# Token lists of the last two batches, and the pace at which w_out is converted in the last layers

## The chip, the cores and the metric

One core of a Trainium2 chip runs the whole program. Its engines are TensorE (PE, matrix products), VectorE (DVE), ScalarE (ACT), GpSimd (POOL), and SyncE (SP), which here only issues DMA. Each engine executes its instructions in the order in which they stand in its own list, and engines wait for each other by semaphores. The metric is the device time of one execution in microseconds (us). TensorE runs at a clock that the chip grants; in the profile "PEclk" 1.00 stands for 2.4 GHz and 0.50 for 1.2 GHz.

## What is computed

Three stages follow each other: attention with pooled keys, a mixture of experts in which every token goes to one expert of limited capacity, and a two-layer network with a squared relu.

```python
# q, k, v: (B=4, H=8, S=576, D=64); keys and values averaged over 8 positions
attn = softmax(q @ k_pooled.T / 8) @ v_pooled
x = attn.transpose(0, 2, 1, 3).reshape(2304, 512)
# moe: E=8 experts, cap=576 tokens each, 512 -> 1024 -> 512
logits = x @ w_gate
expert_idx = argmax(logits, axis=1)          # first come, first served up to cap
h = np.maximum(np.einsum('ecd,edf->ecf', disp, w1), 0.0)
y = np.einsum('ecf,efd->ecd', h, w2)
out[i] = gate_w[i] * y[expert_idx[i], pos[i]]   # tokens that were kept, else 0
# moe2: w_in 512 x 2048 and w_out 2048 x 512 arrive as 64-bit floats
r = np.maximum(x @ w_in, 0.0)
g = s * (r * r) + b
return (g @ w_out).astype(np.float32)
```

## The kernel before, in words

**Order.** The program is scheduled by hand: the order in which the Python code emits instructions is the order of each engine's list. Where several strands of work are woven together, generators are advanced by step tables; no scheduler moves anything afterwards. Every float32 product is made as three matmuls of high and low parts ("h" and "l" tiles): the high part is a cast, the low part a subtraction.

**Attention and routing.** A batch's 576 tokens are five tiles of 128 (the last is half full), in all N = 20 tiles. For a group of tiles `route` (L329) finds each token's expert as a one-hot tile `roh` (L352), and PE then counts the tokens of each expert with matmuls of `roh` and a triangular matrix (L368 to L376, the "ranks"). The rank of a token in its expert is `rr` (L384). `tail` (L397) turns ranks into list positions: `rslot` (L402), `rkey` (L404), the token numbers `tok` (an iota on POOL, L401, masked on DVE, L405), and the one-hot tiles `ohq` (L408, L412) and `ohp` (L414). `add_lists` (L429) multiplies `ohp` and `ohq` on PE (L434) and adds the result to the lists of tokens per expert, `u_lists` (L437). The last batch is routed in two groups: its first three tiles, then its last two. A pick (L689 on PE, L690 and L691 on DVE) reads the list of the next unit of expert work, and POOL gathers that unit's tokens with indirect DMA (`xg`, L938). Expert units of 288 tokens begin while attention still runs: `beside` (L974) lays their layer 1 (L961) and layer 2 (L1108) between the last attention tiles. `w1l` (L930) is the low part of an expert's weights, made on POOL and DVE.

**Conversion of 64-bit weights.** `Weights64` (L850) turns a piece of 128 rows and 512 columns of 64-bit floats into float32 in four steps, each with one DVE instruction: a shift (L868, a tensor_scalar), then three scalar_tensor_tensor instructions (L871, L873, L877). The absolute value `c_u` that the fourth needs is made on ACT (L870) in the second step. The second step of the next piece also finishes the piece before: ACT casts the high part (L1386) and DVE subtracts (L1387); the third step adds the piece into a running sum of all pieces, `raw[3]` (L1392). `w_in` is converted this way earlier, with raw pieces in three tiles `c_raw`; `w_out` has 16 pieces, `wo0` to `wo15`: 14 in a first series of 59 steps, then two in a series of 11.

**Last layers** (`last_layers`, L1362). Units of CU = 256 tokens go through layer 1 (16 column groups f, 12 matmuls of 256 columns each, L1034) and layer 2 (L1432, per f six matmuls of 512 columns). After layer 1 of an f, `square` (L1411 relu on ACT, L1412 on DVE) frees the PSUM bank, and `parts` makes `gh` on ACT (L1426) and `gl` on POOL, or on DVE for every third f (L1427). There are eight banks for unit 0 and four for unit 1. Units 0 and 1 run as a pair (`pair`, L1460) in this order:

- `first(0, 0, 16)`: layer 1 of unit 0, one conversion step per f; in the middle the input of unit 1 is split (`y1l`, L1027);
- `first(1, 0, 7)`: layer 1 of unit 1 up to f = 6 (HEAD = 7), one step per f;
- `second(0, 0, 7)` and `second(1, 0, 7)`: layer 2 of both for f = 0 to 6, two steps per f;
- the rest of `first(1, ...)`, the steps that the first series still has, then the rest of `second` for both with two steps per f.

Then units 2 and on follow one after the other. The first four f of unit 0 (EARLY = 4) are put before the pair, behind the last small expert.

**The hand-over.** The last small expert ends in `last` (L1297): its output `yo` goes from ACT to DRAM by a DMA that SP issues (L1113), and SP then issues the loads of `wo` (L1458). The `wo` tiles lie in pools that are only free once the expert stage has ended.

## Time and profile before

| | |
|---|---|
| three runs | 657.16, 660.01, 661.97 us (median 660.01) |
| the profiled execution | 664.05 us, of which the span of instructions is 662.3 us |
| PE busy | 592.1 us (89%) |
| DVE, ACT, POOL busy | 365.5 us (55%), 253.6 us (38%), 265.8 us (40%) |
| clock granted to PE, mean over the span | 0.952 |
| stages by the trace | attention to about 150 us, experts to about 335 us, last layers from there |

PE is busy nearly all the time, so the time is made of PE's work, of the places where PE waits, and of the stretches in which PE works at half its clock. A row of a timeline gives the start, the busy time, the engine, the line, the operation with its tiles, and in square brackets how long the engine sat idle before and what ended that.

### The profile page before, as it was taken

What the parts mean: (1) busy time and instruction counts of PE and PEld (TensorE: products, weight loads), DVE (VectorE), ACT (ScalarE), POOL (GpSimd) and SP (SyncE); (2) the same over time, 40 slices, a digit from 0 to 9 for tenths busy, and PEclk for the clock granted to TensorE, in tenths of its full rate; (3) what the DMA queues carried; (4) which work ended last, traced back from release to release, by engine and by line L of the source; (5) the groups of instructions that cost most, each with busy time, mean ns of one, the idle gap of its engine ahead of it and who ended that gap; (6) DMA issues with size and microseconds to landing.
All of it is one profiled execution on the core that took longest, in us unless ns stands there. A gap on an engine that the chain in (4) does not pass through costs nothing. (4 is left out here: it accounts for less than half of the span.)

```text
span 662.3 us, 11174 instructions
## 1 busy us (share of the span) xinstructions
PE 592.1 (89%) x4005; PEld 549.5 (83%) x4005; DVE 365.5 (55%) x889; ACT 253.6 (38%) x620; POOL 265.8 (40%) x384
## 2 busy tenths in 40 slices
PE   5787888769899979997897996999999999999884
PEld 5787777669899979996897976889899899898784
DVE  4688798867968956661639999603312021131140
ACT  1354555436456645442336524304125033042130
POOL 5658434715154716012214301305725145144281
PEclk8799899879999989996999898999999999999998
DMA  8989665645649894844548111017300101000000
GB/s 165 199 183 190 163 195 171 215 126 197 232 155 295 282 309 148 282 135 156 169 142 350 38 33 32 1 33 286 111 17 1 49 17 29 29 9 2 35 2 20
DMA packets 67951, 86.12 MB, mean 130 GB/s; under 512 B 24713, under 2 KB 40073, under 8 KB 67856
## 3 DMA queue, kind: packets, MB, share of 16 engines
q1 hardware_dynamic: 57696, 71.34, 35.9%
q10 hardware_dynamic: 7712, 6.84, 3.4%
q0 software_dynamic: 2448, 6.82, 3.1%
q8 instruction: 42, 0.69, 0.5%
q14 instruction: 53, 0.43, 0.2%
HBM read 68.09 MB, written 17.58 MB: 129 GB/s over the span
## 5 line engine op out<-in xcount | busy, mean ns | idle before, releaser
L1432 PE MATMUL bank<-wo,gh 128*128 128x512 f32 (+1 forms) x412 | 119.3, 374 | 1.2 <-ACT wo L1386 1.0
L1427 POOL TENSOR_TENSOR gl<-rt,gh 128x256 fp32r<-128x256 f32 (+1 forms) x96 | 72.6, 761 | 110.8 <-ACT gh L1426 64.7
L1432 PEld LDWEIGHTS bank<-wo,gh 128*128 128x128 f32 x412 | 74.9, 188 | 15.1 <-ACT wo L1386 1.4
L1432 PE MATMUL bank<-wo,gl 128*128 128x512 f32 (+1 forms) x206 | 76.8, 373 | 0.0
L930 POOL TENSOR_TENSOR w1l<-kraw,w1h 128x128 fp32r<-128x128 f32 x96 | 52.6, 582 | 50.7 <-ACT w1h L923 50.6
L1108 PE MATMUL bank<-hs,w2h 128*128 128x288 f32 (+1 forms) x308 | 68.5, 311 | 4.7 <-issue 4.3
L1439 DVE SCALAR_TENSOR_TENSOR raw<-bank,sb,c_u 128x512 f32<-128x512 f32 (+1 forms) x14 | 9.9, 710 | 85.5 <-PE bank L1432 85.5
L1108 PEld LDWEIGHTS bank<-hs,w2h 128*128 128x128 f32 x308 | 50.7, 192 | 5.6 <-issue 5.1
L1411 ACT ACTIVATE rt<-tq 128x256 f32<-128x256 f32 (+1 forms) x26 | 9.5, 367 | 113.5 <-PE tq L1034 91.3
L1108 PE MATMUL bank<-hs,w2l 128*128 128x288 f32 (+1 forms) x148 | 44.7, 302 | 0.0
L1432 PEld LDWEIGHTS bank<-wo,gl 128*128 128x128 f32 x206 | 38.8, 188 | 6.8
L1412 DVE SCALAR_TENSOR_TENSOR rt<-bank,rt 128x256 f32<-128x256 f32 (+1 forms) x53 | 21.2, 401 | 38.3 <-ACT rt L1411 37.9
L1426 ACT CAST gh<-rt 128x256 fp32r<-128x256 f32 (+1 forms) x96 | 36.6, 381 | 6.5 <-DVE rt L1412 6.5
L938 POOL DMA_INDIRECT xg<-xd,u_idx x23 | 25.4, 1104 | 30.0 <-DVE r L288 16.7
L1440 POOL DMA_INDIRECT out_dram<-raw,it x12 | 12.0, 1001 | 62.6 <-DVE raw L1439 62.1
L1411 ACT ACTIVATE rt<-bank 128x256 f32<-128x256 f32 (+1 forms) x60 | 22.3, 371 | 35.4 <-PE bank L1034 27.0
L228 PE MATMUL sc<-kbd,qT 128*128 128x144 f32 (+1 forms) x152 | 25.4, 316 | 5.6 <-DVE r L286 3.6
L1412 DVE SCALAR_TENSOR_TENSOR rt<-tq,rt 128x256 f32<-128x256 f32 (+1 forms) x24 | 9.6, 400 | 36.3 <-ACT rt L1411 36.3
L1108 PEld LDWEIGHTS bank<-hs,w2l 128*128 128x128 f32 x148 | 28.4, 192 | 0.0
L228 PEld LDWEIGHTS sc<-kbd,qT 128*128 128x128 f32 (+1 forms) x152 | 21.9, 201 | 7.7 <-issue 5.1
L934 DVE TENSOR_TENSOR w2l<-vraw,w2h 128x512 fp32r<-128x512 f32 x39 | 27.4, 702 | 1.2 <-ACT w2h L933 0.5
L961 PE MATMUL bank<-xs,w1h 128*128 128x288 f32 (+1 forms) x120 | 26.1, 303 | 2.1 <-DVE hs L964 2.1
(485 smaller groups left out, 1705.0 us busy)
## 6 DMA issues: line engine op xcount, KB each, us to landing
kraw<-in_moe_w_dram SPq DMA_DIRECT2D x14, 1024.0 KB
vraw<-in_moe_w_dram SPq DMA_DIRECT2D x14, 1024.0 KB
wo<-in_moe_w_out_dram SPq DMA_DIRECT2D x16, 512.0 KB
c_raw<-in_moe_w_in_dram ACTq DMA_DIRECT2D x13, 512.0 KB
kraw<-in_k_dram SPq DMA_DIRECT2D x8, 576.0 KB
out_dram<-c_u SPq DMA_DIRECT2D x1, 4608.0 KB
q<-in_q_dram SPq DMA_DIRECT2D x16, 256.0 KB
xd<-xr SPq DMA_DIRECT2D x16, 256.0 KB
```

The costliest lines, as they stand in the source:

```text
L228: nc.tensor.matmul(sc[:n, p // 2, p % 2 * 144:p % 2 * 144 + 144], lhsT=q[:, p, :n], rhs=kbd[b % 2][:, p], start=True, stop=True)
L930: eng.tensor_sub(self.w1l[:, i, z], self.w1(i)[:, z], self.w1h[:, i, z])
L934: eng.tensor_sub(self.w2l[i], self.w2r[:, i], self.w2h[i])
L938: self.nc.gpsimd.indirect_dma_start(out=dst, out_offset=None, in_=self.xd[:have], in_offset=bass.IndirectOffsetOnAxis(ap=idx[:n], axis=0), ...
L961: self.nc.tensor.matmul(p, lhsT=l[:, f, k], rhs=r[k], start=n == 0, stop=n == 3 * KD - 1)
L1108: nc.tensor.matmul(py[d][:, :v.n], lhsT=l[f][:, d * P:d * P + P], rhs=r[f], start=f == 0 and i == 0, stop=f == KF - 1 and i == 2)
L1411: nc.scalar.activation(r, p, AF.Relu)
L1412: nc.vector.scalar_tensor_tensor(out=p if inside else r, in0=p, scalar=0.0, in1=r, op0=ALU.max, op1=ALU.mult)
L1426: nc.scalar.copy(h[:, :n], r)
L1427: (nc.gpsimd if p is None else nc.vector).tensor_sub(l[:, :n], r, h[:, :n])
L1432: nc.tensor.matmul(p[:, c], lhsT=g[:, j * P:j * P + P], rhs=wo[f][:, z, c], start=f == 0 and i == 0, stop=f == KF2 - 1 and i == 2)
L1440: i = nc.gpsimd.indirect_dma_start(out=dst, out_offset=bass.IndirectOffsetOnAxis(ap=ids, axis=0), in_=o[:, c], in_offset=None, bounds_chec ...
```

## The change

**Routing.** The token numbers of all tiles are made once at the start (`toks`), so the iota in `tail` goes. The tail of batch 2 no longer hands its lists over at the first opportunity but waits until tile N - 1; its `add_lists` takes the place of the pick for unit 1, and that pick and its gather move one place on, behind the ranks of the last two tiles. The ending loop gives the second share of side work to the first of the last ranks, not to the second.

**w_in and w_out.** The raw tiles of `w_in` and the first three `wo` pieces share three tiles of a new pool `keep`, so these pieces can be loaded before the expert stage has ended. The last raw piece of `w_in` is loaded at step 51, not 54. In `last`, ACT takes over SP's part in storing the last small expert's output (it loads the address into a register of its own and issues the DMA), and the split of unit 0's input comes two f later.

**Last layers.** For pieces 0 to 2 the absolute value is made on DVE and the high part (and the start of the running sum) on POOL, so that ACT has no part in them. The first 12 steps stand ahead of unit 0's layer 1. Beside it a step is made every second f; in the first half of layer 2 one step per f, where there were two. The steps made by the last square of unit 1 are then 12 + 8 + 7 + 14 + 9 = 50 of 70 (before: 16 + 7 + 28 + 8 = 59); 20 stand behind it (before: 11).

```diff
@@ constants
+        toks = one.tile([P, B, NB], F32, name="toks")
+        nc.gpsimd.iota(toks, pattern=[[S, B], [P, NB]], base=0, channel_multiplier=1, allow_small_or_imprecise_dtypes=True)
@@ tail
-            nc.gpsimd.iota(tok, pattern=[[P, w]], base=b * S + t0 * P, channel_multiplier=1, allow_small_or_imprecise_dtypes=True)
...
-            v.scalar_tensor_tensor(out=tok, in0=r, scalar=float(cap), in1=tok, op0=ALU.is_lt, op1=ALU.mult)
+            v.scalar_tensor_tensor(out=tok, in0=r, scalar=float(cap), in1=toks[:, b, t0:t1], op0=ALU.is_lt, op1=ALU.mult)
...
+            while b == B - 2 and now[0] < N - 1:
+                yield True
             yield from window()
             add_lists(b, at_pe[0])
@@ ending loop
-                    for _ in range(2 if ranks == 1 else 1):
+                    for _ in range(2 if ranks == 0 else 1):
@@ Weights64.step
-                self.nc.scalar.activation(u, t.bitcast(F32)[:, :, 1], AF.Abs)
+                if i < self.alone:
+                    v.tensor_scalar(out=u.bitcast(I32), in0=hi, scalar1=0x7FFFFFFF, scalar2=None, op0=ALU.bitwise_and)
+                else:
+                    self.nc.scalar.activation(u, t.bitcast(F32)[:, :, 1], AF.Abs)
@@ Experts
-            self.c_raw.append(self.m.tile([P, DM, 2], I32, name=f"c_raw{i - 9}"))
+            self.c_raw.append(self.keep.tile([P, DM, 2], I32, name=f"c_raw{i - 9}"))
@@ conv (w_in)
-                    if pos[0] == 3 or pos[0] % 4 == 2 and pos[0] > 6:
-                        self.load_raw(max(3, pos[0] // 4 + 2), queue)
+                    if pos[0] in (3, MARK - 1) or pos[0] % 4 == 2 and 6 < pos[0] < MARK:
+                        self.load_raw(KF2 - 1 if pos[0] == MARK - 1 else max(3, pos[0] // 4 + 2), queue)
@@ last
+            nc.vector.memset(self.ids_half[:, 0:1], 0)
+            nc.scalar.copy(self.ids_half[:, 1:2], self.ids_half[:, 0:1])
+            col = nc.values_load(ti[0:1, 2, self.t.NV + s:self.t.NV + s + 1], engines=[ET.Activation], min_val=0, max_val=T)
...
-                if early and f in (4, 5):
+                if early and f in (6, 7):
...
-            store_small(s)
+            store_y(sid(s), yo(s % 2, SM), SM, nc.scalar, col)
@@ last_layers
-    gl = pool.tile([P, KF2, CU], F32R, name="gl")
-    wo = [pool.tile([P, DM, 2], I32, name=f"wo{i}") for i in reversed(range(KF2))][::-1]
+    gl = side.tile([P, KF2, CU], F32R, name="gl")
+    FIRST = len(x.c_raw)
+    place_out = lambda i, shape, dt: x.keep.tile(shape, dt, name=f"c_raw{i}") if i < FIRST else side.tile(shape, dt, name=f"wo{i}")
+    wo = [place_out(i, [P, DM, 2], I32) for i in reversed(range(KF2))][::-1]
...
-        nc.scalar.copy(w[:, 0], f)
+        if i < FIRST:
+            nc.gpsimd.tensor_copy(w[:, 0], f)
+        else:
+            nc.scalar.copy(w[:, 0], f)
...
-            nc.scalar.copy(raw[3], f)
+            nc.gpsimd.tensor_copy(raw[3], f)
@@ pair
-                conv(1, steps_of_first)
+                conv(u or f % 2, steps_of_first)
...
-                conv(2, end)
+                conv(1 if f < HEAD else 2, end)
...
+        conv(4 * FIRST)
+        nc.gpsimd.memset(onesf, 1.0)
         first(0, 0, KF2, ps)
```

The order in three places, all on DVE. The first is the routing of the last batch: from the list position of its first three tiles to the one-hot tile `roh` of its last two (`xr`, `r`, `lt`, `lg` belong to the attention of the last tile). Before:

```order
L404 TENSOR_SCALAR rkey_1698<-rslot_1696 128x3
L405 SCALAR_TENSOR_TENSOR tok_1699<-rr_1691,tok_1699 128x3
L294 TENSOR_REDUCE lg_174<-lt 64x8
L408 TENSOR_TENSOR ohq<-rkey_1698,q_179 128x144
L409 TENSOR_SCALAR rlo_1697<-rkey_1698 128x3
L411 TENSOR_TENSOR rlo_1697<-rlo_1697,rslot_1696 128x3
L412 TENSOR_TENSOR ohq<-ohq,tok_1699 128x144
L414 TENSOR_TENSOR ohp<-rlo_1697,p_180 128x288
L324 TENSOR_SCALAR xr_176<-xr_176,rgs_1659 128x512
L338 TENSOR_REDUCE rmx_1718<-lg_174 128x2
```

The same place of the change, with the rows that lead to `roh`:

```order
L290 RECIPROCAL r<-r 64x8
L292 TENSOR_TENSOR xr_179<-sc,r 64x512
L294 TENSOR_TENSOR lt<-sc,r 64x64
L296 TENSOR_REDUCE lg_177<-lt 64x8
L326 TENSOR_SCALAR xr_179<-xr_179,rgs_1632 128x512
L340 TENSOR_REDUCE rmx_1695<-lg_177 128x2
L343 TENSOR_TENSOR rd_1697<-lg_177,rmx_1695 128x16
L348 SCALAR_TENSOR_TENSOR rval_191<-rd_1697,rev 128x2x8
L351 TENSOR_REDUCE rvm_1701<-rval_191 128x2
L354 TENSOR_TENSOR roh_1703<-rval_191,rvm_1701 128x16
```

The tail's instructions no longer stand among them: they come some 20 rows further on, behind `roh` and behind the ranks.

The second place is the start of unit 0's squares on DVE, behind the last rows of the expert stage. Before, conversion and squares alternate from the first square on (`rt`, `bank`, `tq` and `misc` are the squares' tiles):

```order
L1412 SCALAR_TENSOR_TENSOR rt_1968<-tq,rt_1968 128x256
L868 TENSOR_SCALAR c_f_16943<-wo_16963 128x512
L1412 SCALAR_TENSOR_TENSOR rt_1969<-misc,rt_1969 128x256
L871 SCALAR_TENSOR_TENSOR c_f_16943<-wo_16963,c_f_16943 128x512
L1412 SCALAR_TENSOR_TENSOR bank_1942<-bank_1942,rt_1970 128x256
L873 SCALAR_TENSOR_TENSOR c_f_16943<-wo_16963,c_f_16943 128x512
```

In the change 18 conversion rows stand ahead of the first square; the last six of them and the first three squares:

```order
L871 TENSOR_SCALAR c_f_17063<-c_raw_17081 128x512
L874 TENSOR_SCALAR c_u_17065<-c_raw_17081 128x512
L877 SCALAR_TENSOR_TENSOR c_f_17063<-c_raw_17081,c_f_17063 128x512
L1400 TENSOR_TENSOR c_raw_17124<-c_f_17064,c_raw_17124 128x512
L879 SCALAR_TENSOR_TENSOR c_f_17063<-c_raw_17081,c_f_17063 128x512
L1405 TENSOR_TENSOR raw_1963<-raw_1963,c_f_17064 128x512
L883 SCALAR_TENSOR_TENSOR c_f_17063<-c_u_17065,c_f_17063 128x512
L1425 SCALAR_TENSOR_TENSOR rt_1968<-tq,rt_1968 128x256
L1425 SCALAR_TENSOR_TENSOR rt_1969<-misc,rt_1969 128x256
L871 TENSOR_SCALAR c_f_17064<-wo_17080 128x512
L1425 SCALAR_TENSOR_TENSOR bank_1942<-bank_1942,rt_1970 128x256
```

So the first square now waits for the conversion of three pieces, and fewer conversion rows lie between the squares that follow.

The third place is DVE behind the last square of unit 1 (its last `gl` is the row with `raw<-bank,raw`), while PE does the second half of layer 2. Before, 12 rows finish the last two pieces:

```order
L1427 TENSOR_TENSOR raw_16984<-bank_1942,raw_16984 128x256
L868 TENSOR_SCALAR c_f_16943<-wo_17514 128x512
L871 SCALAR_TENSOR_TENSOR c_f_16943<-wo_17514,c_f_16943 128x512
L873 SCALAR_TENSOR_TENSOR c_f_16943<-wo_17514,c_f_16943 128x512
L877 SCALAR_TENSOR_TENSOR c_f_16943<-c_u_16945,c_f_16943 128x512
L868 TENSOR_SCALAR c_f_16944<-wo_17516 128x512
L871 SCALAR_TENSOR_TENSOR c_f_16944<-wo_17516,c_f_16944 128x512
L1387 TENSOR_TENSOR wo_17702<-c_f_16943,wo_17702 128x512
```

In the change 11 rows stand between that `gl` and the last two pieces:

```order
L1440 TENSOR_TENSOR raw_17104<-bank_1942,raw_17104 128x256
L879 SCALAR_TENSOR_TENSOR c_f_17063<-wo_17071,c_f_17063 128x512
L1405 TENSOR_TENSOR raw_1963<-raw_1963,c_f_17064 128x512
L883 SCALAR_TENSOR_TENSOR c_f_17063<-c_u_17065,c_f_17063 128x512
L871 TENSOR_SCALAR c_f_17064<-wo_17070 128x512
L877 SCALAR_TENSOR_TENSOR c_f_17064<-wo_17070,c_f_17064 128x512
L1400 TENSOR_TENSOR wo_17786<-c_f_17063,wo_17786 128x512
L879 SCALAR_TENSOR_TENSOR c_f_17064<-wo_17070,c_f_17064 128x512
L1405 TENSOR_TENSOR raw_1963<-raw_1963,c_f_17063 128x512
L883 SCALAR_TENSOR_TENSOR c_f_17064<-c_u_17065,c_f_17064 128x512
L1400 TENSOR_TENSOR wo_17792<-c_f_17064,wo_17792 128x512
L1405 TENSOR_TENSOR raw_1963<-raw_1963,c_f_17064 128x512
```

The pieces `wo12` and `wo13` are thus finished here too, ahead of `wo14` and `wo15`.

## Rows read from the trace of the kernel before

**Rows 1.** The page: busy time of each engine (share of the span), instructions

```profile
PE 592.1 (89%) x4005; PEld 549.5 (83%) x4005; DVE 365.5 (55%) x889; ACT 253.6 (38%) x620; POOL 265.8 (40%) x384
```

**Rows 2.** Timeline of DVE in the routing: start, busy, instruction, idle before

```profile
130.49 0.15 DVE L404 TENSOR_SCALAR rkey<-rslot 128x3 f32<-128x3 f32 x1
134.75 0.16 DVE L405 SCALAR_TENSOR_TENSOR tok<-rr,tok 128x3 f32<-128x3 f32 x1 [4.11 <-POOL tok L401]
...
136.08 0.48 DVE L324 TENSOR_SCALAR xr<-xr,rgs 128x512 f32<-128x512 f32 x1
...
137.29 0.17 DVE L352 TENSOR_TENSOR roh<-rval,rvm 128x16 bf16<-128x16 f32 x1
```

**Rows 3.** Timeline of PE in the routing

```profile
119.33 1.15 PE L434 MATMUL o<-ohp,ohq 128*48 128x96 f32 x10 [1.00 <-DVE ohp L414]
...
131.86 0.29 PE L961 MATMUL misc<-xs,w1l 128*128 128x288 f32 x1
137.52 0.20 PE L368 MATMUL o<-roh,tri 128*128 128x16 bf16 x1 [5.37 <-DVE roh L352]
...
152.29 0.41 PE L952 MATMUL tq<-ident,xg 96*128 96x96 f32 x3
```

**Rows 4.** Tile xg: gathers (ns min/median/max, first and last start), and issue to landing

```profile
L938 POOL DMA_INDIRECT xg<-xd,u_idx x23: 923/985/2147, 105.0 to 302.8; - x23
...
DMA to landing us min/median/max: 3.1/5.0/7.1
```

**Rows 5.** Windows of 2 us: busy of PE, PEld, DVE, ACT, POOL; PEclk; DMA

```profile
366.00:368.00 2.00, 2.00 (x11) 2.00 (x11) 1.54 (x5) 1.08 (x4) 0.74 (x1) 0.50 0.64 194
```

**Rows 6.** Timeline of SP at the hand-over to the last layers

```profile
328.09 1.04 SPq L1022 DMA_DIRECT2D it<-idc  x1
...
339.62 3.93 SPq L1458 DMA_DIRECT2D wo<-in_moe_w_out_dram  x6
```

**Rows 7.** Timeline of DVE at the hand-over, and beside POOL's gl

```profile
332.60 1.43 DVE L1027 TENSOR_TENSOR yhl<-yr,yhl 128x256 fp32r<-128x256 f32 x4 [7.66 <-ACT yhl L1026]
...
344.11 0.43 DVE L868 TENSOR_SCALAR c_f<-wo 128x512 int32<-128x512 int32 x1 [6.63 <-DMA wo<-in_moe_w_out_dram]
...
349.62 1.23 DVE L1387 TENSOR_TENSOR wo<-c_f,wo 128x512 fp32r<-128x512 f32 x1
```

**Rows 8.** Timeline of DVE: conversion alone, and behind the last square

```profile
400.03 0.69 DVE L1387 TENSOR_TENSOR wo<-c_f,wo 128x512 fp32r<-128x512 f32 x1 [0.24 <-ACT wo L1386]
400.63 0.68 DVE L873 SCALAR_TENSOR_TENSOR c_f<-wo,c_f 128x512 int32<-128x512 int32 x1
...
418.10 0.42 DVE L1412 SCALAR_TENSOR_TENSOR rt<-bank,rt 128x256 f32<-128x256 f32 x1 [0.33 <-ACT rt L1411]
418.44 0.41 DVE L1427 TENSOR_TENSOR raw<-bank,raw 128x256 fp32r<-128x256 f32 x1
...
426.53 0.69 DVE L1387 TENSOR_TENSOR wo<-c_f,wo 128x512 fp32r<-128x512 f32 x1 [0.80 <-issue]
```

**Rows 9.** Timeline of PE in the last layers

```profile
346.27 0.40 PE L1034 MATMUL tq<-yhl,w2h 128*128 128x256 f32 x2
...
363.85 0.58 PE L1034 MATMUL tq<-y1l,w1h 128*128 128x256 f32 x1 [2.63 <-DVE y1l L1027]
...
406.10 0.39 PE L1034 MATMUL bank<-y1h,w2h 128*128 128x256 f32 x1 [3.79 <-DVE rt L1412]
...
409.56 0.58 PE L1034 MATMUL tq<-y1h,w2h 128*128 128x256 f32 x1 [1.77 <-DVE gl L1427]
```

**Rows 10.** The chain that ended last: start, length, engine, tile, line

```profile
417.64 24.59 PE bank L1432 x108
442.24 1.42 PE tq L1034 x12
```

**Rows 11.** Timeline of POOL: a gl beside DVE, a 512-column op on POOL

```profile
295.42 1.27 POOL L1046 TENSOR_TENSOR w2l<-raw,w2h 128x512 fp32r<-128x512 f32 x1 [5.65 <-ACT w2h L1045]
...
349.37 0.92 POOL L1427 TENSOR_TENSOR gl<-rt,gh 128x256 fp32r<-128x256 f32 x1 [1.01 <-ACT gh L1426]
```

More of the change, by code (lines that the diff above doesn't have):

```diff
@@ L852, with __init__ @@
 class Weights64:
-    def __init__(self, nc, pieces, raw, out, f, u, late=None):
-        self.nc, self.raw, self.out, self.f, self.u, self.late = nc, raw, out, f, u, late
+    def __init__(self, nc, pieces, raw, out, f, u, late=None, alone=0):
+        self.nc, self.raw, self.out, self.f, self.u, self.late, self.alone = nc, raw, out, f, u, late, alone
         self.pieces, self.total = pieces, 4 * pieces + (3 if late else 2)
@@ L887, in __init__ @@
             self.n, self.xh, self.xl, self.hh, self.hl = n, x[:KD], x[KD:2 * KD], h[:KF], h[KF:2 * KF]
-    def __init__(self, nc, tc, c, a, left, m, xd, idc, yt, hist, cap, capp):
+    def __init__(self, nc, tc, c, a, left, keep, m, xd, idc, yt, hist, cap, capp):
         self.__dict__.update({k: v for k, v in locals().items() if k != "self"})
@@ L1076, in main @@
         queue = nc.scalar
-        c_f = [one.tile([P, DM], I32, name=f"c_f{i}") for i in range(2)]
+        c_f = [left.tile([P, DM], I32, name=f"c_f{i}") for i in range(2)]
         def out(i, f):
@@ L1086, in main @@
         cv = Weights64(nc, KF2, lambda i: self.c_raw[i % 3], out, lambda i: self.raw[i].bitcast(I32) if i < KF else c_f[i % 2],
-                       [one.tile([P, DM], F32, name=f"c_u{i}") for i in range(2)])
+                       [(left, one)[i].tile([P, DM], F32, name=f"c_u{i}") for i in range(2)])
         NU, cap, capp = self.t.NU, self.cap, self.capp
@@ L1108, in layer2, with store_y @@
                     nc.tensor.matmul(py[d][:, :v.n], lhsT=l[f][:, d * P:d * P + P], rhs=r[f], start=f == 0 and i == 0, stop=f == KF - 1 and i == 2)
-        def store_y(u, y, n):
+        def store_y(u, y, n, queue=nc.sync, col=None):
             for d in range(KD):
                 nc.scalar.copy(y[:, d], py[d][:, :n])
-            nc.sync.dma_start(out=self.yt.rearrange("(d p) n -> p d n", p=P)[:, :, cols(u, n)], in_=y)
+            queue.dma_start(out=self.yt.rearrange("(d p) n -> p d n", p=P)[:, :, bass.ds(regs[u][1] if col is None else col, n)], in_=y)
         def store_unit(u, v=self.v):
@@ L1359, in main, with last_layers @@
         rest_small(1)
-def last_layers(nc, tc, c, a, pool, x, ps, out):
+def last_layers(nc, tc, c, a, pool, side, x, ps, out):
     NV = -(-T // CU)
@@ L1372, in last_layers @@
     x.yp.append(y)
-    cf, cu = [pool.tile([P, DM], I32, name=f"c_f{i}") for i in range(2)], [pool.tile([P, DM], F32, name="c_u0")]
+    cf, cu = [x.w.tile([P, DM], I32, name=f"c_f{i}") for i in range(2)], [x.w.tile([P, DM], F32, name="c_u0")]
     gh = pool.tile([P, KF2, CU], F32R, name="gh")
-    gl = pool.tile([P, KF2, CU], F32R, name="gl")
-    wo = [pool.tile([P, DM, 2], I32, name=f"wo{i}") for i in reversed(range(KF2))][::-1]
+    gl = side.tile([P, KF2, CU], F32R, name="gl")
+    FIRST = len(x.c_raw)
+    place_out = lambda i, shape, dt: x.keep.tile(shape, dt, name=f"c_raw{i}") if i < FIRST else side.tile(shape, dt, name=f"wo{i}")
+    wo = [place_out(i, [P, DM, 2], I32) for i in reversed(range(KF2))][::-1]
     ph, po = ps[0:4], ps[4:8]
@@ L1384, in split_out @@
     def split_out(i, f):
-        w = wo[i] = pool.tile([P, 2, DM], F32R, name=f"wo{i}")
-        nc.scalar.copy(w[:, 0], f)
+        w = wo[i] = place_out(i, [P, 2, DM], F32R)
+        if i < FIRST:
+            nc.gpsimd.tensor_copy(w[:, 0], f)
+        else:
+            nc.scalar.copy(w[:, 0], f)
         nc.vector.tensor_sub(w[:, 1], f, w[:, 0])
@@ L1467, in pair @@
                     nc.sync.dma_start(out=sb[:, j:j + 1], in_=a[n].unsqueeze(0).to_broadcast([P, 1]))
-        more.extend(pool.tile([P, 2, 2, CU], F32R, name=f"wo{i}") for i in range(KF2 - 2, KF2))
+        more.extend(side.tile([P, 2, 2, CU], F32R, name=f"wo{i}") for i in range(KF2 - 2, KF2))
         spare.extend(x.w.tile([P, 2, CU], F32R, name=f"raw{i}") for i in range(3))
         held = []
-        nc.gpsimd.memset(onesf, 1.0)
         def first(u, f0, f1, banks):
@@ L1500, in pair @@
         for i in range(KF2 - 2, KF2):
-            wo[i] = pool.tile([P, DM, 2], I32, name=f"wo{i}")
+            wo[i] = place_out(i, [P, DM, 2], I32)
             load_out(i)
@@ L1509, in pair @@
         raw[0:3] = [x.w.tile([P, DM], F32, name=f"raw{i}") for i in range(3)]
-        slots.extend(raw[2:4] + [pool.tile([P, DM], F32, name="c_f1")])
-        sums["drop"] = pool.tile([P, DM], F32, name="c_u0")
+        slots.extend(raw[2:4] + [x.w.tile([P, DM], F32, name="c_f1")])
+        sums["drop"] = x.w.tile([P, DM], F32, name="c_u0")
     def unit(u):
@@ L1609, in program @@
                     x.main(w, m1, ps)
+            side = es.enter_context(tc.tile_pool(name="s", bufs=1, side="right"))
             pool = es.enter_context(tc.tile_pool(name="n", bufs=1))
-            last_layers(nc, tc, c, a, pool, x, ps, out)
+            last_layers(nc, tc, c, a, pool, side, x, ps, out)
 def kernel(**inputs):
```

8 lines of the change are left out of this document (4 added, 4 removed).

## The prediction

> **What bounds the kernel now.** I read the page first: PE is busy 592.1 us, 89% of the span [rows 1], so little but PE's own waits can be won. Then the timeline of PE, for its idle times and what ended them, and the windows of 2 us, for the granted clock. In the part that the change touches three places stand out. At the last ranks PE finishes a layer-1 matmul at 132.15 and starts L368 only at 137.52, 5.37 us idle, released by `roh` [rows 3]. In the pair of the last layers it waits for the fourth `y1l` (2.63 us), and 3.79 and 1.77 us at f = 7 of unit 1, for DVE's squares [rows 9]. After each of these places PE runs at half clock: six windows read like the one in [rows 5], PE busy 2.00 and PEclk 0.50 (1.2 GHz): one from 138, three from 364, two from 410. Work that fills such a window takes 1 us at 2.4 GHz, so each costs 1 us. All three waits end with DVE, so DVE's timeline in those stretches came last.
>
> **Routing.** DVE stands 4.11 us before `tok` (L405), released by POOL's iota [rows 2]. `roh`, on which PE waits, is in the queue behind it. The change takes the iota away, and moves the tail's six small instructions behind `roh`. From `tok` at 134.75 to the next row of the attention at 136.08 is 1.33 us, nearly all of it the tail's: I let 1.25 us leave the path [rows 2]. The addition to the lists comes in ahead, with its matmuls where the pick's one matmul stood: I take 0.6 us, an estimate from the 1.15 us of ten such matmuls at 119.33 [rows 3], less the pick and what lies beside DVE's other work. So `roh` starts at 137.29 - 4.11 - 1.25 + 0.6 = 132.5, and L368 at about 132.8 (0.23 us later, as now); PE is free at 132.15 + 0.6 = 132.75 [rows 2, 3]. The wait goes; L368 comes 4.7 us earlier. With it should go the half clock behind it (1 us for the window from 138, and 0.7 for parts of its neighbours). What comes back: the PE wait for `ohp` at the last additions, now later in the list (0.4, the bare wait of such a place), and about 1 us where weights of the next expert arrive no earlier than now, since their DMA goes on at its own pace. 4.7 + 1.7 - 1.4 = 5.0. **I take -5.0**; the bounds are 0 (everything comes back at the next weights) and -6.5 (nothing does).
>
> The pick of unit 1 moves behind the ranks, so its three gathers start near 134. One takes POOL 0.99 us, and the slowest landed 7.1 us after issue [rows 4], so all three are there by about 144. PE first reads them at 152.29 [rows 3], less 5: 147.3. Covered by 3 us; if that cover went, each us late would be a us of PE. Waiting with batch 2's lists costs nothing by itself: no pick before unit 1's reads them.
>
> **Last layers: the head.** Now SP has the store of `yo` ahead of the loads and issues `wo0` only at 339.62; DVE gets it at 344.11, 4.5 us later, after 6.63 us idle [rows 6, 7]. In the change SP has nothing left to wait for after its load at 328.09, and the tiles of pieces 0 to 2 are those of `w_in`'s raw pieces, long read. Loaded from 329.1, they are there by 333.6. DVE ends its split of unit 0's input at 334.03 [rows 7] and starts the 12 steps: 18 rows, six tensor_scalar (0.43, [rows 7]) and twelve long ones, which follow each other at 0.60 (400.03 to 400.63, [rows 8]): 2.6 + 7.2 = 9.8. I add 1.7 for waits on POOL's casts, whose price on a 512-column tile no row shows: between 0.24, the wait for ACT's cast [rows 8], and 1.27 each, a 512-column subtraction on POOL [rows 11]; near the middle, three times 0.57. First square at 345.5. That is late: PE has its eight banks full and needs the first one back at 346.27 [rows 9], where today it needs no wait. The square ends at 345.9, so 0.4 us are left.
>
> Then DVE has a step every second f, and the fourth `y1l`, which releases PE now at 363.85, comes after 14 squares, 4 `y1l` and 4 `gl` (0.34 apart, as 418.10 and 418.44 [rows 8]) and 11 conversion rows: 7.5 + 6.3 = 13.8, plus some 1.7 of stretching by POOL (three times the 0.54 below): 361.0, which is 2.8 us earlier. I let the wait of 2.63 shrink to 0.8 only, since a part of the 2.8 is taken up by the three `y1l` ahead of it, for which PE waits in turn: -1.8. The three windows at half clock that follow I count as half gone: -1.5.
>
> **Last layers: the middle.** Per f of layer 2 PE needs 24.59 / 18 = 1.37 us [rows 10]. A step with its share of subtraction and addition is (5 x 0.60 + 0.43 + 0.4 of waits) / 4 = 0.95 us. Now 28 steps (26.7 us) stand beside 14 x 1.37 = 19.1 us: DVE comes out late, and the squares of f = 7 on stand behind it. With 14 steps it needs 13.3 us and is done first. The waits of 3.79 and 1.77 go, and with them the two half-clock windows and some 1 us of partial ones: -8.6.
>
> **Last layers: the end.** 20 steps remain after the last square. Layer 2 goes on at 417.64; the last `gl` is DVE's at 418.44, 0.8 + 0.4 = 1.2 us in [rows 8, 10]. From there 18 rows lead to the low half of `wo14`: 15 long ones (9.0), three short (1.3), and the waits for ACT's cast, 0.24 twice and 0.80 once where nothing fills it [rows 8]: 11.6. So `wo14` is there 12.8 us in; PE wants it after seven f, at 9.6: a wait of 3.3. `wo15` comes 3.3 later, PE is back after 1.37: 1.9 more. That is 5.2 us of new waits, 5.6 with releases. Half clock behind them I take at 2 us (behind the two waits of 5.56 it was 3, behind 3.79 alone, at 406.10, the matmul still took 0.39). +7.6.
>
> Sum: -1.8 - 1.5 - 8.6 + 7.6 = **-4.3**: unit 2 starts at 437.9 instead of 442.24 [rows 10], before the gain of routing; bounds -10.5 (no wait at the end) and +1 (the head's price at its upper end, half clock kept).
>
> **Edits at nothing.** The earlier load of the last raw `w_in` piece and the two-f later split lie beside PE work that needs neither; if the split were late, PE's first f of unit 0 would wait for it, by up to the 1.43 us that it takes [rows 7]. ACT's register load and store wait on work that ACT now awaits as well; what is queued behind are the first squares' relus, needed only at 345.5. The new pools change addresses alone.
>
> **A rule against it.** Where DVE's subtraction L1387 at 349.62 meets a `gl` on POOL at 349.37 (0.92), it takes 1.23 instead of 0.69 [rows 7, 8, 11]. By the rows a DVE instruction with two inputs loses 0.54 beside such a POOL instruction; three on 512 columns in the lead would cost at most 3 x 1.27 = 3.8.
> The Trainium skill, "SBUF — State Buffer", section "Who interferes with whom", says that such a DVE instruction and a GpSimd one that reads SBUF block each other outright for a whole instruction, by issue order. Row and rule agree in sign; by the rule the lead would take the 3.8 in full.
>
> **Rivals.**
> 1. *POOL blocks the lead.* Three blocks of 1.27: the lead ends at 334.03 + 9.8 + 3.8 = 347.6, the bank is free at 348.0, PE waits 1.8 there and stays at half clock after the `y1l` (1.5). 650.7 + 3.3 = 654. For: the 1.23 above. Against: no other POOL work there.
> 2. *Only half holds.* Routing's gain is lost again at the next weights, or the end eats the last layers' gain: 660 - 4.3 to 660 - 5.0, about 655.4. For: nothing in the change brings those weights earlier, and the 5.2 us at the end are worked out from bare rows.
> 3. *All of it, and more.* PE's clock never falls at the end or behind `y1l`, and nothing comes back in the routing: 650.7 - 2 - 1.5 - 1.4 - 1.5 (the lead without POOL's 1.7) = 644.3.
> 4. *Slower.* `wo0` lands as late as now, 344.11. Then the lead ends at 344.1 + 11.5 = 355.6 and PE waits 355.6 + 0.4 - 346.3 = 9.7 us in unit 0, with 2 us of half clock: last layers -4.3 + 11.7 = +7.4; routing -5 or, lost too, 0: 662 to 667. The point that decides: SP's load issued before 341 costs less than the gain. For: the load waits for the tiles' last readers and for SP; against: both are free before 330.
> 5. *No change*: the lists are not what DVE stands for, and the steps only move: 660.
>
> **How the numbers follow.** The sum is -9.3, on the profiled execution 664.05 to 654.75. That execution is 4 us above the median of the runs (660.01), so from the median **650.7**. Chances: forecast 0.44, rival 1 0.10, rival 2 0.22, rival 3 0.14, rival 4 0.05, rival 5 0.05. The range runs from rival 3 to a little beyond rival 2, 643 to 658; what it leaves out is rivals 4 and 5 and tails. About 1% is what a measurement tells from no change, 653.4 and 666.6 here. Faster takes the forecast, rival 3, and a part of rivals 1 and 2: 0.62; slower, the upper part of rival 4 and a tail, 0.05; the rest, 0.33, is within 1%.
>
> **What would show it.** Routing: `tok` with no idle before it, L368 near 133. Head: the first `wo` load on SP near 329, 18 conversion rows on DVE from 334, the first square near 345.5 less the shift, no PE wait at the ninth f. Middle: PE without waits at f = 7 of unit 1. End: PE waits of some 3.3 and 1.9 us for `wo14` and `wo15`. It is wrong if the load comes late, if the lead is stretched, or if PE loses the routing's gain before 200 us.

## The result, and the profile after

The changed kernel takes 652.57 us (median of 13 runs), the kernel before 658.08 us (13 runs on the same chips); the ratio is 0.9917, 95% interval 0.9896 to 0.9938, which is 5.5 us less (4.1 to 6.8). The point forecast, from a median of 660.01, was 9.3 us less. The profiled execution of the change is a short one (649.31 us, span 647.6), that of before was a long one (664.05), so the two traces must not simply be subtracted; below stand two profiles of each.

The routing, timeline of PE after the change (start, busy, instruction, idle before and what ended it):

```profile
122.19 0.74 PE L958 MATMUL tq<-ident,xg 96*128 96x96 f32 x3 [5.91 <-DVE xs L960]
...
131.02 0.18 PE L370 MATMUL o<-roh,tri 128*128 128x16 bf16 x1
...
132.24 0.33 PE L692 MATMUL o<-u_small,u_lists 48*96 48x4 f32 x2 [0.92 <-DVE hist L382]
```

The ranks (L370, L368 before) start at 131.02 without a wait, where they started at 137.52 after 5.37 us [rows 3]. The wait of 5.91 before L958 stood at 2.89 before; the list addition that filled part of it (1.15 us at 119.33, [rows 3]) has moved behind it, and the half clock now lies behind this wait: the mean PEclk by the windows is 0.68 from 120 to 130 and 1.00 from 130 to 140, where it was 0.83 and 0.73. A short wait for the pick (0.92) is new.

Why DVE stood so long before `tok` in the kernel before is seen in its timeline of POOL: the iota itself takes 0.24 us, but it is in the queue behind three gathers of some 0.97 us each.

```profile
131.02 0.99 POOL L938 DMA_INDIRECT xg<-xd,u_idx  x1 [1.43 <-DVE rkey L404]
...
133.59 0.97 POOL L938 DMA_INDIRECT xg<-xd,u_idx  x1 [0.30 <-issue]
134.57 0.24 POOL L401 IOTA tok<- 128x3 f32 x2
```

The hand-over after the change, in the timelines of SP, DVE and POOL:

```profile
317.57 1.30 SPq L1471 DMA_DIRECT2D c_raw<-in_moe_w_out_dram  x3
```

```profile
323.24 0.43 DVE L871 TENSOR_SCALAR c_f<-c_raw 128x512 int32<-128x512 int32 x1 [1.71 <-DMA c_raw<-in_moe_w_out_dram]
...
326.31 0.83 DVE L874 TENSOR_SCALAR c_u<-c_raw 128x512 int32<-128x512 int32 x1
327.06 1.09 DVE L877 SCALAR_TENSOR_TENSOR c_f<-c_raw,c_f 128x512 int32<-128x512 int32 x1
...
330.34 0.84 DVE L874 TENSOR_SCALAR c_u<-c_raw 128x512 int32<-128x512 int32 x1
...
334.11 0.41 DVE L1425 SCALAR_TENSOR_TENSOR rt<-tq,rt 128x256 f32<-128x256 f32 x1
...
337.58 1.20 DVE L1400 TENSOR_TENSOR c_raw<-c_f,c_raw 128x512 fp32r<-128x512 f32 x1 [0.51 <-POOL c_raw L1397]
...
340.30 1.23 DVE L1405 TENSOR_TENSOR raw<-raw,c_f 128x512 f32<-128x512 f32 x1
...
351.42 0.41 DVE L1033 TENSOR_TENSOR y1l<-yr,y1h 128x256 fp32r<-128x256 f32 x1
```

```profile
326.18 0.68 POOL L1397 CAST c_raw<-c_f 128x512 fp32r<-128x512 f32 x1 [11.09 <-ACT rt L1424]
326.82 0.79 POOL L1407 COPY raw<-c_f 128x512 f32<-128x512 f32 x1
330.15 0.74 POOL L1397 CAST c_raw<-c_f 128x512 fp32r<-128x512 f32 x1 [2.54 <-DVE c_f L883]
...
339.96 1.01 POOL L1440 TENSOR_TENSOR gl<-rt,gh 128x256 fp32r<-128x256 f32 x1 [1.73 <-ACT gh L1439]
```

SP issues the first load right behind its own last one, as forecast, but the data land 5.7 us later (323.24 - 317.57), not 4.5, so DVE waits 1.71. The lead takes 10.87 us (323.24 to 334.11), 1.07 more than its bare 9.8. Three rows in it are stretched, each beside a cast or the copy on POOL: 0.83 and 0.84 for 0.43, 1.09 for 0.69.

The last layers, timeline of PE, and the window of 2 us behind the longest wait (columns as in [rows 5]):

```profile
334.57 0.50 PE L1040 MATMUL tq<-yhl,w2h 128*128 128x256 f32 x2 [0.44 <-DVE rt L1425]
339.17 0.50 PE L1040 MATMUL bank<-yhl,w2h 128*128 128x256 f32 x2 [1.59 <-DVE gl L1440]
351.88 0.58 PE L1040 MATMUL tq<-y1l,w1h 128*128 128x256 f32 x1 [2.56 <-DVE y1l L1033]
...
404.52 0.50 PE L1445 MATMUL bank<-wo,gh 128*128 128x512 f32 x1 [0.90 <-ACT wo L1399]
405.25 0.50 PE L1445 MATMUL bank<-wo,gh 128*128 128x512 f32 x1 [0.23 <-DVE wo L1400]
...
409.64 1.58 PE L1445 MATMUL bank<-wo,gh 128*128 128x512 f32 x2 [2.97 <-ACT wo L1399]
...
413.72 0.49 PE L1445 MATMUL bank<-wo,gh 128*128 128x512 f32 x1 [0.25 <-DVE wo L1400]
```

```profile
410.00:412.00 2.00, 2.00 (x5) 1.30 (x5) 2.00 (x4) 0.00 (x0) 0.00 (x0) 0.50 0.00 0
```

The waits at f = 7 of unit 1 (3.79 and 1.77 us, [rows 9]) are gone. In their place stand 0.90 and 0.23 us for the two halves of `wo13` and 2.97 us for `wo14`, with half clock behind that; `wo15` costs 0.25 more. The wait for the fourth `y1l` is what it was (2.56, before 2.63), and the head of unit 0 has two new waits (0.44 and 1.59) for squares and a `gl` behind the lead.

### The profile page after: what moved, and what is told of

Its sections match the earlier page's. It is cut to its first block, busy times and chain, and to the rows that moved or that the text cites. A ratio compares the mean times of both kernels' runs of the same rounds, so it can differ in the third digit from the quotient of the medians.

```text
span 647.6 us, 11182 instructions
## 1 busy us (share of the span) xinstructions
PE 587.1 (91%) x4005; PEld 541.5 (84%) x4005; DVE 366.6 (57%) x893; ACT 249.4 (39%) x614; POOL 265.5 (41%) x384
## 5 line engine op out<-in xcount | busy, mean ns | idle before, releaser
L1440 POOL TENSOR_TENSOR gl<-rt,gh 128x256 fp32r<-128x256 f32 (+1 forms) x96 | 70.1, 735 | 94.1 <-ACT gh L1439 76.4
L1445 PE MATMUL bank<-wo,gh 128*128 128x512 f32 (+1 forms) x340 | 101.4, 381 | 4.3 <-ACT wo L1399 3.9
L1445 PEld LDWEIGHTS bank<-wo,gh 128*128 128x128 f32 x340 | 62.5, 189 | 19.1 <-ACT wo L1399 5.5
L1445 PE MATMUL bank<-wo,gl 128*128 128x512 f32 (+1 forms) x170 | 64.2, 378 | 0.0
L1445 PEld LDWEIGHTS bank<-wo,gl 128*128 128x128 f32 x170 | 32.2, 189 | 6.4
L230 PE MATMUL sc<-kbd,qT 128*128 128x144 f32 (+1 forms) x152 | 23.9, 302 | 4.7 <-DVE rmine L380 3.2
L275 PE MATMUL o<-vx,eT 128*128 128x146 f32 (+1 forms) x144 | 23.5, 309 | 3.1 <-DVE lt L294 2.5
```

Of the source, the lines that this page charges most:

```text
L230: nc.tensor.matmul(sc[:n, p // 2, p % 2 * 144:p % 2 * 144 + 144], lhsT=q[:, p, :n], rhs=kbd[b % 2][:, p], start=True, stop=True)
L1440: (nc.gpsimd if p is None else nc.vector).tensor_sub(l[:, :n], r, h[:, :n])
L1445: nc.tensor.matmul(p[:, c], lhsT=g[:, j * P:j * P + P], rhs=wo[f][:, z, c], start=f == 0 and i == 0, stop=f == KF2 - 1 and i == 2)
```

## The experiments

Five marks cut each trace into stages: the value matmul with a wait of 0.73 us near 109 (A), the expert matmul L952 (L958 after) behind a 1.1 us wait near 180 (B), the first row of the first small expert (D, 302.68 before), the 32 matmuls of the last small expert (E, 327.05), layer 2 of unit 2 (U, 465.88, the row of 96 matmuls in the chain), and the last matmul's wait (H, 626.01). Each figure comes from one execution and scatters by a microsecond or two, A to B by more; in us:

| kernel | A to B | B to D | D to E | E to U | U to H | time, ratio to before |
|---|---|---|---|---|---|---|
| before | 74.3 | 118.5 | 24.4 | 138.8 | 160.1 | |
| before, second profile | 73.5 | 118.8 | 22.6 | 137.9 | 160.2 | 1.0019 (0.9992 to 1.0046) |
| toks_only | 68.9 | 120.2 | 21.8 | 136.5 | 160.1 | 0.9945 (0.9916 to 0.9975) |
| routing_alone | 69.2 | 119.3 | 21.6 | 136.8 | 160.2 | 0.9947 (0.9917 to 0.9976) |
| layers_alone | 75.0 | 117.4 | 21.6 | 138.5 | 161.3 | 0.9987 (0.9956 to 1.0017) |
| changed | 69.0 | 116.4 | 20.5 | 136.4 | 161.2 | 0.9917 (0.9896 to 0.9938) |
| changed, second profile | 68.6 | 117.2 | 21.6 | 136.3 | 161.2 | 0.9918 (0.9882 to 0.9954) |
| pace2 | 70.7 | 118.0 | 20.5 | 130.8 | 160.9 | 0.9807 (0.9770 to 0.9845) |
| old_pace | 72.3 | 116.7 | 21.0 | 134.1 | 161.3 | one execution, 651.26 us |
| mark54 | 72.3 | 119.5 | 22.7 | 145.3 | 161.3 | one execution, 667.78 us |
| mark54_again | 70.7 | 120.4 | 21.3 | 145.3 | 161.4 | 1.0111 (1.0044 to 1.0178) |
| all_left | 69.4 | 116.9 | 20.4 | 137.2 | 161.5 | one execution, 652.02 us |
| pace2_y8 | 69.7 | 117.2 | 20.4 | 129.0 | 161.2 | 0.9815 (0.9782 to 0.9849) |
| pace2_y8_left | 69.4 | 117.6 | 20.5 | 128.3 | 161.2 | 0.9793 (0.9761 to 0.9824) |

E to U once more in parts, by the timelines of PE: the head from E to the first layer 2 of the pair; the middle from there to the second half of layer 2 (layer 2 for f = 0 to 6, then layer 1 of unit 1 from f = 7 on); the end, which is that second half. What is left is layer 1 of unit 2, 23.5 to 23.7 us in all of them.

| kernel | head | middle | end |
|---|---|---|---|
| before; second profile | 48.4; 47.8 | 42.0; 41.7 | 24.6; 24.6 |
| toks_only; routing_alone | 46.4; 47.1 | 41.7; 41.3 | 24.6; 24.6 |
| changed; second profile | 47.8; 47.2 | 32.5; 32.5 | 32.4; 32.9 |
| layers_alone; all_left | 48.4; 47.3 | 32.5; 32.5 | 33.9; 33.5 |
| pace2; old_pace | 47.7; 52.5 | 33.5; 32.9 | 25.9; 25.0 |
| pace2_y8; pace2_y8_left | 46.0; 45.9 | 33.5; 32.9 | 25.8; 25.7 |
| mark54; mark54_again | 54.8; 56.0 | 32.5; 32.4 | 34.3; 33.1 |

### The two halves apart

`routing_alone` is the kernel before with the hunks `constants`, `tail` and `ending loop` of the diff; `layers_alone` is the kernel before with all the others.

> The kernel before with the routing part alone (token numbers made once, list addition of batch 2 moved, pick of unit 1 moved). Theory A (each half of the change brings its own gain): the profile shows no DVE idle before tok, the ranks L370 of the last two tiles without a PE wait, PE about 5.8 us earlier at the list addition that ended at 150.62 before; time 5 to 6 us below before. Rival B (the routing's gain is given back at later weights): the same at 150, but PE's lead over before is under 2 us at 240 and the time is within 2 us of before. Rival C (the gain between 240 and 327 us belongs to the whole change, by a transfer that no longer collides): no such gain here, lead at 327 equal to that at 240.

> The kernel before with all but the routing part (early loads, hand-over through ACT, lead of 12 steps, half pace). Theory A: PE waits at f = 7 of unit 1 gone, waits of about 1.1 and 3 us for wo14 and wo15, from the ninth f of unit 0 to unit 2 about 3 us shorter than before; time 2.5 to 4 us below before. Rival B (the last layers hold all of the net gain of 5.5): 5 to 6 us below. Rival C (a transfer of an expert's weights no longer collides, since the last raw piece of w_in is loaded earlier): 6 to 10 us below, with PE waiting 2 us rather than 4.26 us for kraw near 300 us and no half clock after it.

The routing alone is worth 3.5 us (1.6 to 5.5), less than the 5 to 6 of theory A, and A to B is 5 us shorter; from A to U it takes 346.9 us where the two profiles of before have 356.0 and 352.8, so rival B of that expectation falls. The other half alone is worth 0.9 us, with an interval from 2.9 less to 1.1 more: theory A expected 2.5 to 4, and missed. Its stages show why. B to D is shorter by 1 to 3 us than in the four profiles without it, but the last layers from E to U are as long as before and U to H is 1.1 us longer. In parts the middle is some 9 us shorter, the end as much longer (24.6 to 33.9), and the head has gained nothing. Rival C of that expectation had the right mechanism at kraw (below), not its size.

A to B depends on more than the routing: in the other kernels with the change's routing it is 68.6 to 72.3 us. In `old_pace`, one of the two longest, the windows behind the wait for `xs` are at half clock from 122 to 132, in the changed kernel up to 126.

### Second profiles of both kernels

> The kernel before, unchanged, for a second profile. Theory A (the stretch at half clock from 302 to 312 us after a 4.26 us wait for kraw is an accident of one execution): it is absent or shorter here, and the profiled execution is 3 to 6 us shorter. Rival C (it belongs to the kernel before): PE waits over 3.5 us for kraw near 300 us again, with half clock for 8 us or more behind it.

> The changed kernel, unchanged, for a second profile. Theory A: routing 5.8 us earlier than before at the list addition again; from the ninth f of unit 0 to unit 2 about 93 us; the stretch from 290 to 315 us may be longer than in the first profile by a wait and half clock, since the time of 649.3 us is the lowest of 13. Rival C: no PE wait over 2.5 us and no half clock between 290 and 315 us.

Timeline of PE in the second profile of the kernel before:

```profile
136.17 0.19 PE L368 MATMUL o<-roh,tri 128*128 128x16 bf16 x1 [4.09 <-DVE roh L352]
...
302.12 1.30 PE L1243 MATMUL bank<-rt,vraw 128*128 128x144 f32 x4 [3.94 <-DMA kraw<-in_moe_w_dram]
```

The wait for kraw belongs to the kernel before (3.94 us here, 4.26 in the first profile, 4.04 in `routing_alone`); how long the half clock behind it lasts differs: up to 312 in the first profile, up to 308 here, and D to E is 1.7 us shorter. So each expectation holds in part. Where the last piece of `w_in` is loaded earlier, the row in this place reads:

```profile
294.25 0.97 PE L1248 MATMUL bank<-rt,vraw 128*128 128x144 f32 x6 [2.00 <-ACT w1h L1089]
```

This is the changed kernel; 1.92 in its second profile, 2.12 in `layers_alone`. The wait is half as long, and by the profile it no longer ends with a transfer. Half clock behind it is absent in the first profile of the change and there from 296 to 300 in the second, so that rival C of `after_again` holds for the wait only. This gain I had not forecast.

### Which part of the routing

`toks_only`: the kernel before with the two lines of `toks` and the two changed lines at the top of `tail`; the lists and the pick stay where they were.

> The kernel before with the token numbers made once at the start and nothing else of the routing part (batch 2's lists and the pick for unit 1 stay where they were). Theory A (DVE's wait for POOL's iota is the smaller half of the routing's gain, since the tail's own instructions and the move of the lists stay in the way): no DVE idle before tok, PE still waits 0.5 to 1.5 us for roh, no half clock behind it, and the time is 3 to 5 us below before. Rival (the wait only changes its name, since rkey or another instruction behind POOL's gathers holds DVE as long): PE waits 3 us or more for roh, time within 2 us of before.

Timeline of DVE in `toks_only`:

```profile
130.33 0.15 DVE L405 TENSOR_SCALAR rkey<-rslot 128x3 f32<-128x3 f32 x1
130.40 0.15 DVE L406 SCALAR_TENSOR_TENSOR tok<-rr,toks 128x3 f32<-128x3 f32 x1
...
132.94 0.18 DVE L354 TENSOR_TENSOR roh<-rval,rvm 128x16 bf16<-128x16 f32 x1
```

`tok` follows `rkey` at once, `roh` is made at 132.94 where it was at 137.29, and PE does not wait for the last ranks at all: it comes to them at 133.54, after a stretch at half clock from 126 to 132. The ratio is that of the whole routing part, 0.9945 beside 0.9947. So the gain is the iota's, as far as the two intervals can tell; the moved lists and pick, and `roh`'s further advance of some 2 us (130.78 in the changed kernel), bring nothing that this measurement shows. Counted from A, the last ranks come 3.8 us earlier than in the first profile of before, and 5.4 in the changed kernel, but at B the two are level (68.9 and 69.0): the half clock lies from 126 to 132 here and from 120 to 126 there. Theory A had the time right (3.6 us less, where 3 to 5 were expected) and the two shares the wrong way round.

### The pace of the conversion

```diff
# pace2: two steps per f again in unit 1's first half
-                conv(1 if f < HEAD else 2, end)
+                conv(1 if f < HEAD and u == 0 else 2, end)
# old_pace: the lead stays, the paces are those of before
-                conv(u or f % 2, steps_of_first)
+                conv(1, steps_of_first)
-                conv(1 if f < HEAD else 2, end)
+                conv(2, end)
```

> The changed kernel, but with two steps per f again in the first half of unit 1's layer 2 (one per f stays in unit 0's layer 1's second f and in unit 0's first half of layer 2): 57 steps are made by the last square and 13 stand behind it. Theory A (the waits for wo14 and wo15 and the half clock behind them cost the changed kernel its gain in the last layers, since the lump behind the last square is too long): these waits (0.9 and 3.0 us) are gone, squares at f = 7 of unit 1 let PE wait under 1 us, and the time is 4 to 6 us below the changed kernel's 652.6. Rival (the seven steps only move the wait back to the squares of f = 7): a wait of 3 us or more at f = 7, time within 2 us of the changed kernel's.

> The changed kernel with the paces of before (one step per f beside unit 0's layer 1, two per f in the first half of layer 2), the lead of 12 steps staying. Theory A (the lead delays the squares, and the half pace is what pays for it): the fourth y1l lets PE wait 5 us or more rather than 2.56, and the part from the ninth f of unit 0 to unit 2 is 2 to 6 us longer than the changed kernel's 93. Rival (the pace beside unit 0 does not matter): y1l wait 2 to 3 us, and that part 1 to 3 us shorter, since no lump is left at the end.

Timeline of PE in `pace2`, from the first wait of the pair to unit 2:

```profile
342.37 0.51 PE L1040 MATMUL bank<-yhl,w2h 128*128 128x256 f32 x2 [1.49 <-DVE gl L1440]
355.07 0.58 PE L1040 MATMUL tq<-y1l,w1h 128*128 128x256 f32 x1 [2.56 <-DVE y1l L1033]
...
393.43 0.39 PE L1040 MATMUL tq<-y1h,w2h 128*128 128x256 f32 x1 [1.16 <-DVE gl L1440]
```

`pace2` is 6.6 us faster than the changed kernel by the medians (645.94 us), some 7 by the two ratios. The waits for `wo13` and `wo14` are gone, one of 1.16 us stands at f = 7 of unit 1, and no window from 392 to 416 is at half clock. E to U is 5.6 us shorter than in the changed kernel: the end falls from 32.4 to 25.9, the middle rises by 1.0. Theory A holds, with a wait a little over the 1 us and a gain a little over the 4 to 6 that it named: 20 steps behind the last square are too many, 13 fit, and DVE had room for seven more beside layer 2.

`old_pace`, of which there is one execution, is also faster than the changed kernel from E to U (134.1 against 136.4), though its waits in unit 0 are longer:

```profile
343.29 0.51 PE L1040 MATMUL bank<-yhl,w2h 128*128 128x256 f32 x2 [2.98 <-DVE gl L1440]
...
359.59 0.58 PE L1040 MATMUL tq<-y1l,w1h 128*128 128x256 f32 x1 [2.63 <-DVE y1l L1033]
```

The rival's two figures are met (2.63 us at the `y1l`, 2.3 us less from E to U), but not its reason: the pace beside unit 0 does matter, since the head is 52.5 us long where it is 47.8 and 47.2 in the changed kernel and 46.4 to 48.4 with full pace and no lead. Theory A has that part right, half pace pays for the lead, though not at the `y1l`, where the wait is 2.6 us at either pace: the full pace shows in the 2.98, in three waits ahead of the `y1l` (1.3 us together) and in longer half clock. What `old_pace` wins back is the end, 25.0 us for 32.4.

### The early load of w_in's last piece

```diff
# mark54 and mark54_again
-                    if pos[0] in (3, MARK - 1) or pos[0] % 4 == 2 and 6 < pos[0] < MARK:
-                        self.load_raw(KF2 - 1 if pos[0] == MARK - 1 else max(3, pos[0] // 4 + 2), queue)
+                    if pos[0] == 3 or pos[0] % 4 == 2 and pos[0] > 6:
+                        self.load_raw(max(3, pos[0] // 4 + 2), queue)
```

> The changed kernel with the last raw piece of w_in loaded at step 54 again, as before. Theory A (the 2 us that the changed kernel gains between 240 and 300 us come from that load being issued earlier, ahead of kraw's): PE waits about 4 us for kraw near 294 us instead of 2.0, and that stretch (from the PE row behind the 4 to 5 us wait at 234 to the first row of the small expert) takes 61.5 to 62.4 us instead of 59.7. Rival (it comes from the hand-over or from another part): 59.7 as in the changed kernel.

> mark54 once more, timed: the changed kernel with the last raw piece of w_in loaded at step 54. Theory A (with that load late, SP's first load of w_out waits for the store of the last small expert's output that ACT issues, so the lead starts 10 us late): SP waits over 6 us for that store, the first square is late and PE waits 6 us or more at the ninth f of unit 0, and the time is 8 to 16 us above the changed kernel's 652.6, so slower than before. Rival (the 667.8 us of the one execution was an accident): the first load is issued within 3 us of the store of the changed kernel, time 651 to 657 us.

Timeline of PE in `mark54_again`, the waits of SP (line, what it waited for, us in total, times, longest), and SP's own timeline:

```profile
298.75 1.62 PE L1248 MATMUL bank<-rt,vraw 128*128 128x144 f32 x6 [4.36 <-DMA kraw<-in_moe_w_dram]
...
347.16 0.79 PE L1040 MATMUL tq<-yhl,w2h 128*128 128x256 f32 x2 [8.17 <-DVE rt L1425]
```

```profile
SPq L1471 <- DMA yt<-yo: 9.1, 1, 9.1
```

```profile
331.81 2.15 SPq L1471 DMA_DIRECT2D c_raw<-in_moe_w_out_dram  x3
```

With that load late, all else unchanged, the kernel is slower than before: 1.0111, some 12 us above the changed kernel. The wait for kraw is back (4.36 us, and 4.52 in `mark54`). B to E is 142.2 and 141.7 us in the two kernels with the load late and 140.9 to 142.9 in the four profiles without the change's loads, but 136.9 to 139.0 in the eight with the early load. And the first load of `w_out` now waits 9.1 us for the store of `yo`, which in the change goes from ACT's queue: the early place of the load is what lets SP run ahead of that store. The lead then starts late, and PE waits 8.17 us at the ninth f. That the load's wait covers the store only in this order is shown; which semaphore makes it so is not.

### The place of the tiles and the split of unit 1's input

```diff
# all_left: gl, wo3 to wo15 and the tiles `more` in `pool`, the first three pieces in `keep`
-    gl = side.tile([P, KF2, CU], F32R, name="gl")
+    gl = pool.tile([P, KF2, CU], F32R, name="gl")
...
# pace2_y8: on pace2, unit 1's input split two f earlier
-                if u == 0 and 10 <= f < 10 + KD:
-                    x.split_y(1, f - 10, nc.vector)
+                if u == 0 and 8 <= f < 8 + KD:
+                    x.split_y(1, f - 8, nc.vector)
```

> The changed kernel with gl and the pieces wo3 to wo15 in the pool where they were before (the first three pieces stay in the new pool). Theory A (the place of the tiles sets how fast PE reads them): layer 2 of a later unit, 96 matmuls, takes 21.80 us as before, not 22.20. Rival (the 0.4 us per unit has another cause, such as the pieces 0 to 2): 22.20 again. No other difference is expected by either beyond 3 us of time.

> pace2 with unit 1's input split two f earlier (y1h and y1l at f = 8 to 11 of unit 0, not 10 to 13). Theory A (the fourth y1l is late because it stands behind squares and conversion on DVE, not because its input is late): the 2.56 us wait for it goes, with the half clock behind it, and the time is 2 to 4 us below pace2's 645.9. Rival (squares that now stand behind y1l make PE wait for banks instead): the same sum of waits in unit 1's first four f, time within 1.5 us of pace2's.

> pace2_y8 with gl and the pieces wo3 to wo15 in the pool where they were before. Theory A (the place sets PE's rate in layer 2): 21.99 us or less for 96 matmuls of a later unit instead of 22.20, and some 1 to 2 us less time than pace2_y8, since nine units and both halves of the pair run layer 2. Rival (what layer 2 gains layer 1 loses again, as units of both kernels took 44.4 to 44.6 us in all): time within 0.7 us of pace2_y8's.

The chains of the changed kernel, then of `all_left`, at unit 2's layer 2, where the kernel before has 21.80 us:

```profile
451.18 22.20 PE bank L1445 x96
```

```profile
452.54 21.99 PE bank L1445 x96
```

The same 96 matmuls take 22.20 us in every kernel that has all of the change's pools and 21.80 in every one without them; `all_left` gives half of that back. So where the tiles lie has a part in PE's rate; whether the three pieces in `keep` are the other half was not tried. It costs little, for layer 1 of these units runs the other way: between the layers 2 of units 2 to 5 it takes 22.41, 22.26 and 22.40 us in the changed kernel where it took 22.57, 22.78 and 22.57. Four layers 2 are thus 1.6 us longer and three layers 1 are 0.85 shorter; with a last wait of 2.69 instead of 2.35 us this is the 1.1 us between U and H. In `all_left` layer 1 is back at 22.57 and 22.79, and U to H is no shorter.

`pace2_y8` has 0.9815, no less than `pace2`. The wait for `y1l` is gone, and another has come in its place, in the timeline of PE:

```profile
361.22 0.38 PE L1040 MATMUL bank<-y1h,w1h 128*128 128x256 f32 x1 [2.30 <-DVE raw L1440]
```

The rival holds in the waits (0.44 and 2.30 us here, 2.56 and 0.19 in `pace2`) and in the time: the sum of DVE's work in that stretch is late, and whichever piece stands last has the wait. The head is 1.7 us shorter than in `pace2`, which the time does not show. `pace2_y8_left`, both edits together, is the fastest that ran: 644.37 us, 0.9793; it can't be told from `pace2` or `pace2_y8`. Its layer 2 is at 21.99 us as theory A said, but its layer 1 at 22.57 and 22.78, and U to H is 161.2 us as in `pace2_y8`, which is the rival's reason.

## Why the prediction was right or wrong

**Routing: right in place, near in size, wrong in its parts.** Forecast -5.0, measured 5.3 and 4.9 us in A to B by the two pairs of profiles and 3.5 (1.6 to 5.5) in time. DVE's stand before `tok` was the cause, and the half clock behind the late ranks goes with it. The 1.25 us for moving the tail's instructions bring no more, as `toks_only` shows. The cover for the moved gathers held: PE reads `xg` from 145.47 on without waiting for it. What comes back at the next weights, forecast at about 1 us, can't be told: B to D is 118.5 and 118.8 us before, 119.3 and 120.2 with the routing alone.

**The head: the step that failed.** The early load and the lead came where they were put, and the first square ended 0.44 us too late for PE, where 0.4 us were to be left: the load took 5.7 us to land, not 4.5, while POOL's casts cost 1.07 us, not 1.7. What failed are the -1.8 and -1.5 for the fourth `y1l`. From the first square to the end of that `y1l` I summed 15.5 us of DVE, 1.7 of it for stretching; it took 17.7 (334.11 to 351.83). Five conversion rows beside POOL's `gl` took 1.13 to 1.23 us instead of 0.68, where I had counted three such losses, and the first of them waited 0.51 for POOL's cast. PE waits 1.59 us at a `gl` on the way and still 2.56 at the `y1l`. From E to the fourth `y1l` it is 37.1 and 36.8 us in the changed kernel and 36.8 in both profiles of before. The half clock behind is shorter in the first pair (352 to 355, where it was 364 to 370), but by the heads of four profiles each the change gains nothing: 47.7 us on average, 47.5 without it, instead of 3.3 less.

**The middle: right.** Both waits at f = 7 went, with the half clock behind them; a wait of 1.00 us for a `wo` piece in the first half of layer 2 went too. The middle is 9.1 us shorter on average, forecast 8.6.

**The end: right in mechanism, a little dearer.** The last pieces cost 0.90 + 0.23 + 2.97 + 0.25 = 4.35 us of waits where 5.2 was worked out (the wait for `wo15` fell to 0.25 as PE ran at half clock ahead of it), with some 2 us of half clock. With releases and the slower matmuls the end is 7.8 and 8.3 us longer in the changed kernel's two profiles, 8.6 on average of four; the forecast was 7.6. That this term eats what the middle gains was in the sum; that the pace was chosen too slow, and that two steps per f in unit 1 alone give 6.6 us, I did not see.

**Edits at nothing: wrong in both directions.** I costed the early load of `w_in`'s last piece at nothing. By the stages it brings 2 to 4 us from B to E, since kraw is there in time, and it holds the cover of the whole lead. Rival 4, the slower case, named the late load of `wo0` and priced its wait at 9.7 us; `mark54_again` shows 8.17, from a condition that I had thought free. That the new pools change addresses alone was right as a reason and wrong as a price: layer 2 takes 22.20 instead of 21.80 us per unit. Layer 1 gives most of it back; it is part of the 1.1 us after U.

**The sum.** -9.3 was made of -5.0 and -4.3. Measured are -5.5 in all; alone, the routing brings 3.5 and the rest 0.9, with intervals that leave room for the difference. In the rest, 2 to 4 us from the early load stand against 1.1 us after U, and the last layers up to U bring about nothing: -9.1 in the middle, +8.6 at the end. That is rival 2, "the end eats the last layers' gain", nearer than the forecast: 655.4 from a median of 660.01, 4.6 less. That the time still lies where the range had it is in part luck, since a gain that I had not forecast stands in for the head's.
